# Six block pairs by eleven products, and gate products laid among the output sums, in a convolution and SwiGLU kernel

## The chip, the cores and the metric

The kernel runs on one core of one Trainium2 chip. The metric is the device time of one execution in microseconds (us). Engines are named as the profile names them: PE is TensorE's matmul stream and PEld its weight loads, DVE is VectorE, ACT is ScalarE, POOL is GpSimd, SP issues nearly all DMAs. PSUM, the memory that PE writes, is used as four pairs of banks; the code calls such a pair a duo.

## The reference, cut to what matters

```python
# x: (8, 4096, 192), weight: (8 heads, 7 taps)
w = softmax(weight, axis=-1)                     # with 1e-9 in the divisor
conv[b, s, h, g] = sum over k of w[h, k] * x_padded[b, s + k, h, g]   # causal, 6 zeros ahead
# then, with all 32768 rows of conv as tokens:
xn  = conv / sqrt(mean(conv * conv, axis=-1) + 1e-6) * rms_g
g   = xn @ w_gate                                # 192 x 1536
silu = g / (1 + exp(-g))
out = (silu * (xn @ w_val)) @ w_out              # 1536 x 192
```

All in float32. The weights arrive as float64.

## The kernel before

**Tiles and stages.** The 32768 tokens are cut into 32 *pairs* of 1024 tokens (the name `p` in the code; two groups of 512 tokens). Pair 0 and, in its gate half, pair 1 are computed by ordinary products while the weights are converted and prepared; pairs 2 to 31 run in one steady pattern. For each pair there is work ahead of the products (seven convolution taps on DVE and ACT, the norm, a turn through DRAM that puts channels on the partitions), the gate and value products, the SiLU and its multiply, and the output product.

**Gate and value products.** The 1536 hidden columns are cut into six *block pairs* `j`, each of two blocks of 128. For a block pair and the two token groups there are four results, the cells a, b, c, d. Rows 0 to 63 of the array do the gate and rows 64 to 127 the value, each with 64 of the 192 channels at a time, so a cell by the ordinary way takes three such products and the four cells take twelve. `FORM` (L71) says of each block pair which way it goes: 1 is a form with eleven products, named P1 to P7 and Q1 to Q4; 0 is the ordinary form with twelve, named Aa to Ed. Each product is six matmuls of 512 columns: three parts of a float32 operand split by hand into fp32r parts, times the two row halves (`product`, L898, issued at L910). The eleven-product form needs sums on top of the products: `f1` copies cell a to cell b in PSUM (ACT), `f3` copies cell c to two rows of the tile `tt` (ACT), `f4` and `f5` write c and d as b plus that copy (DVE, L981). P6 adds to b after `f1`; `f4` reads b after P6; P7 adds to b after `f4` has read it; `f5` reads b after P7; Q2 and P3 add to c after `f4`, Q4 to d after `f5`, Q3 and P4 to b after `f5`. Then `g` applies SiLU to a cell's gate bank (ACT, L987) and `m` multiplies by its value bank (DVE, L994).

**Output product.** It is done by seven products instead of eight for 2x2 blocks, with sums of the hidden values first (`h1` to `h4`, 24 a pair, shared between DVE and POOL, L964). For each of the seven forms and each block pair there is one step, `o1.0` to `o7.5`, 42 a pair (`step`, L918, issued at L937): six matmuls with 32 weight columns each, side by side in the array. They add up in three accumulators X, Y and Z, which a few copies, sums and transposes (`c1`, `c2`, `s7`, `C21`, `C22`, `T11` to `T22`) turn into output rows. Each accumulator took a duo of its own.

**Weights.** The prepared weight pieces of the gate stage lie in DRAM (`wd`, made by `prepare`, L733, in `NW` = 10 kinds) and come back for every pair through a ring of ten slots of 192 KB (`ring_load`, L782). A slot is loaded again as soon as its last product has been issued: 48 loads a pair.

**Order.** Nothing reorders the work: every engine does its instructions in the order in which Python issues them, and that order is written by hand. `LINE` (L111) lists PE's steps for one pair. `ORDER` (L79) is one *window* of the steady state and is run once for each pair (`run`, L1245; L1269). In `ORDER`, `p4` means the next four steps of `LINE`; a word such as `Vf4.0` means engine V (DVE; A is ACT, G is POOL, S a DMA on SP's queue) and act `f4` of block pair 0. A `+` behind a word means the next pair, `++` the one after it, `-` the pair before, nothing means the window's own pair. `cv` are the taps, `sq`, `red`, `pow`, `bc`, `mul` the norm, `x1` to `x4` sums of the split operands, `n`, `d`, `l` the splits into fp32r parts, `pl`, `ft`, `ld`, `st` the DMAs. `FIRST` (L95) is the window of pair 1 and `PLAIN` (L75) its PE steps. In a window of before, PE does the pair's P5.0 and P1.0, the last six output steps of the pair before, then the other 66 gate products of the pair in a row, then 36 of its own output steps in a row.

**Banks.** `open` (L849) takes a free duo and `give` (L857) returns it when a cell's `g` and `m` have read their halves.

Of the kernel before, what the change touches and what calls it, by code (L numbers as in the profile page):

```python
# [20 lines left out]
def kernel(  # L21
# [46 lines left out]
    SPAN = 1509  # L68
    SPLIT = 2.0**-12
    HIGH = 0xFFFFF000  # L70
    FORM = (1, 0, 1, 0, 1, 1)  # L71
    HOME = tuple(
        sum(FORM[:j]) if on else sum(FORM) + j - sum(FORM[:j]) for j, on in enumerate(FORM)
    )
    PLAIN = (  # L75
        "a0 b0 c0 d0 o1.0 a1 b1 c1 d1 o1.1 a2 b2 c2 d2 o1.2 a3 b3 c3 d3 o1.3 a4 b4 c4 d4 o1.4",
        "a5 b5 c5 d5",
    )
    ORDER = (  # L79
# [14 lines left out]
    )  # L94
    FIRST = (  # L95
# [14 lines left out]
    )  # L110
    LINE = (  # L111
# [7 lines left out]
    )  # L119

    cst = ctx.enter_context(tc.tile_pool(name="cst", bufs=1))
# [8 lines left out]
    x_sb = {}  # L130
# [30 lines left out]

    def load_part(p, h, eng):

        if h == 0:
            x_sb[p] = xs.tile([P, TB + HALO, GS], F32, name="xh")
        load_head(p, p // NB, (p % NB) * PT, h, eng)

# [505 lines left out]
    def copy(eng, dst, src):  # L673
        if eng == "A":
            nc.scalar.copy(out=dst, in_=src)  # L675
        else:
            nc.vector.tensor_copy(out=dst, in_=src)
# [32 lines left out]
    for k, (name, cols) in enumerate((("A", (0, 9)), ("B", (5, 7)), ("E", (1, 3)))):  # L710
        for c, (g, f) in CELL.items():
            OWN[name + c], RIGHTS[name + c], INTO[name + c] = (k, g), cols[f], c
    NW = 10
    NSLOT = 10

    line_of = [w.split(".") for row in LINE for w in row.split()]
# [119 lines left out]
    class Pair:  # L836
        def __init__(self, p):
            self.p = p
            self.bk, self.o_sb, self.sg = {}, {}, {}
            self.open_half, self.turned = {}, [0, 0]  # L840
            self.line = self.products()

        def hv(self, j, c):
# [13 lines left out]
        def give(self, name, n=1):  # L857
            self.open_half[name] = self.open_half.get(name, 0) + n
            if self.open_half[name] == 2:
                pool4.append(self.bk.pop(name))  # L860
                del self.open_half[name]

        def both(self, j, c):
            return duo[self.bk[j, c]][:]

        def acc(self, b):
            return duo[self.bk[b]][:, 0, :]

        def products(self):
            if self.p == 1:  # L870
# [46 lines left out]

        def step(self, form, k):  # L918
            b = ACC[form]
            if form in (1, 7) and b not in self.bk:  # L920
                full4.discard(self.open(b, False))
            fresh = form in (1, 7) and k == 0
            src = hs[:, k, :] if form == 5 else self.hv(k, LEFT[form])
            right = RIGHT[form][:, HOME[k]]
            self.tiles(b, [right[:, m] for m in range(NM)], src, fresh)
# [40 lines left out]
        def do(self, eng, name):  # L966
            act, *at = name.split(".")
            p, n = self.p, NM * P
            s5 = tt[:, 7:9, :]
            if at:  # L970
                j = int(at[0])
            if act == "f1":
                self.open((j, "b"), True)
                copy(eng, self.both(j, "b"), self.both(j, "a"))
            elif act == "f3":
                copy(eng, s5, self.both(j, "c"))
            elif act in ("f4", "f5"):
                c = "c" if act == "f4" else "d"
                if c == "d":
                    self.open((j, c), True)  # L980
                nc.vector.tensor_tensor(  # L981
                    out=self.both(j, c), in0=self.both(j, "b"), in1=s5, op=ALU.add
                )
            elif act[0] == "g":
                c = act[1]
                t = self.sg[j, c] = spots.pop(0)
                nc.scalar.activation(  # L987
                    out=tt[:, t, :], in_=self.both(j, c)[:, 0, :], func=AF.Silu
                )
                self.give((j, c))  # L990
            elif act[0] == "m":
                c = act[1]
                t = self.sg.pop((j, c))
                nc.vector.tensor_tensor(  # L994
                    out=self.hv(j, "abcd".index(c)), in0=self.both(j, c)[:, 1, :],
                    in1=tt[:, t, :], op=ALU.mult,
                )
                self.give((j, c))
                spots.append(t)
            elif act[0] == "h":  # L1000
                self.h_sum(int(act[1]), j, eng)
            elif act == "c1":
                self.open("Y", True)
                copy(eng, self.some("Y"), self.some("X"))
            elif act in ("s7", "c2"):
                i, b = (7, "Z") if act == "s7" else (8, "X")
                copy(eng, tt[:, i, 0:n], self.some(b))
            elif act in ("C22", "C21"):
                i, b = (7, "X") if act == "C22" else (8, "Z")
                t = tt[:, i, 0:n]  # L1010
                nc.vector.tensor_tensor(out=t, in0=self.some(b), in1=t, op=ALU.add)  # L1011
                if b == "Z":
                    self.give("Z", 2)
            elif act in ("T22", "T21"):
                self.turn(tt[:, 7 if act == "T22" else 8, :], 1, int(act[2]) - 1)
                self.at_end(1)
            elif act in ("T11", "T12"):
                b = "Y" if act == "T11" else "X"
                self.turn(self.acc(b), 0, int(act[2]) - 1)
                self.give(b, 2)  # L1020
                self.at_end(0)
            elif p < PAIRS - 1:
                self.leave(int(act[2]), j, eng)
# [24 lines left out]
        tap(p, k, eng)  # L1048

    def put_away(p, h, eng):  # L1050
        if h == 0:
            scr[p] = dram.tile([D, PT], F32, name="xd")
        to = scr[p][:].rearrange("(h a) (b t) -> h b a t", a=GS, t=TB)
        queue(eng).dma_start(out=to[h], in_=yn[p][h::H])
# [210 lines left out]
                    pairs[p].do(eng, name)  # L1265

    run([w for row in FIRST for w in row.split()], 1)
    for w in range(2, PAIRS + 1):
        run([w for row in ORDER for w in row.split()], w)  # L1269
# [1 line left out]
_INS = ['x', 'weight', 'moe_w_gate', 'moe_w_val', 'moe_w_out', 'moe_rms_g']  # L1271
# [26 lines left out]
```

## Time and profile before

| | before |
|---|---|
| time, median of 3 runs | 2475.02 us (2474.97 to 2477.09) |
| span of the profiled execution | 2476.6 us |
| granted PE clock over the span | 0.999 |
| instructions in the profile | 69229 |
| DMA packets, bytes | 716392, 430.55 MB |
| time of one steady window (start of a tap to the same tap one pair later) | 74.75 us |

The profiled execution's span stands 1.6 us above the median of the timed runs and inside their range. In the profile, "busy" is the time in which an engine had an instruction in flight; matmuls overlap each other, so PE's busy share tells whether PE had work, not how fast it did it. A group's row gives the busy time, the mean length of one instruction, and the idle time just before its instructions with what ended it. The chain of waits follows the work that ended last back from the end. A timeline row gives start, length, engine, line, what is written from what, and how many instructions were merged into the row.

### The profile page before, as it was taken

The numbers are of one execution on the slowest core, as the hardware profiler recorded it, in microseconds if no ns is written. First come the engines' busy times: TensorE is split into PE (matmuls) and PEld (weight loads), VectorE is DVE, ScalarE is ACT, GpSimd is POOL, SyncE is SP. The second block draws the span as 40 slices with busy tenths as digits, with TensorE's granted clock in tenths as the row PEclk, the third lists the DMA queues.
The fourth block names the chain that finished last, engine by engine and source line by source line (L and its number), as shares of the span: only waits on it lengthen the run. The fifth ranks groups of instructions, "written<-read, shape, count | busy, mean of one in ns | idle before, by whom it ended". The sixth has DMA issues, their size and how long they took to land.

```text
span 2476.6 us, 69229 instructions
## 1 busy us (share of the span) xinstructions
PE 2454.1 (99%) x29152; PEld 1896.0 (77%) x29152; DVE 2020.8 (82%) x2526; ACT 1018.0 (41%) x1435; POOL 836.2 (34%) x624
## 2 busy tenths in 40 slices
PE   8999999999999999999999999999999999999999
PEld 5546777877777877777787778777777877778777
DVE  8687888888888888888888887888888888888864
ACT  6443344434344334344334444343444343443332
POOL 0541333333333333334233434333433333333322
PEclk9999999999999999999999999999999999999999
DMA  7363677666687666786666777666776666876653
GB/s 151 60 205 107 171 200 194 190 161 175 173 205 185 189 162 173 176 211 178 177 167 171 191 193 191 173 167 172 199 198 187 160 172 172 205 185 192 159 162 94
DMA packets 716392, 430.55 MB, mean 174 GB/s; under 512 B 510330, under 2 KB 702386, under 8 KB 716082
## 3 DMA queue, kind: packets, MB, share of 16 engines
q1 hardware_dynamic: 712336, 425.21, 66.4%
q8 instruction: 230, 3.77, 0.7%
q10 hardware_dynamic: 3746, 0.92, 0.2%
q14 instruction: 80, 0.66, 0.1%
HBM read 366.96 MB, written 58.98 MB: 172 GB/s over the span
## 4 chain that ended last, share of the span: by engine, by line
PE 92%; DVE 4%; DMA 2%; issue 1%; ACT 1%; POOL 0%; SPq 0%; DVEq 0%; POOLq 0%; ACTq 0%
PE ps L910 54%; PE ps L937 35%; PE ps L882 2%; DMA xb<-xd 1%; DMA ring<-wd 1%; DVE y L445 0%; DVE ht L1109 0%; PE ps L408 0%; DVE ht L994 0%; DVE ps L981 0%; PE ps L528 0%; DVE part L345 0%; DVE part L330 0%; DVE ht L964 0%; ACT part L675 0%
## 5 line engine op out<-in xcount | busy, mean ns | idle before, releaser
L910 PE MATMUL ps<-part,ring 64*128 64x512 f32 x12240 | 1419.9, 389 | 3.4 <-DMA ring<-wd 2.3
L910 PEld LDWEIGHTS ps<-part,ring 64*128 64x128 f32 x12240 | 1151.3, 184 | 258.4 <-DVE ps L981 12.0
L987 ACT ACTIVATE tt<-ps 128x512 f32<-128x512 f32 x744 | 439.3, 599 | 714.5 <-PE ps L910 661.2
L994 DVE TENSOR_TENSOR ht<-ps,tt 128x512 f32<-128x512 f32 x744 | 497.7, 686 | 254.8 <-ACT tt L987 252.3
L937 PE MATMUL ps<-ht,wo_sb 128*32 128x384 f32 (+2 forms) x7272 | 468.3, 380 | 1.9 <-DVE tt L1011 1.1
L964 POOL TENSOR_TENSOR ht<-ht 128x512 f32<-128x512 f32 x180 | 273.6, 1527 | 541.6 <-PE ps L937 534.1
L937 PE MATMUL ps<-ht,x 128*32 128x384 f32 (+2 forms) x6696 | 440.3, 380 | 2.9 <-DVE ht L964 2.9
L937 PEld LDWEIGHTS ps<-ht,wo_sb 128*32 128x32 f32 x7272 | 325.0, 110 | 115.8 <-issue 14.8
L937 PEld LDWEIGHTS ps<-ht,x 128*32 128x32 f32 x6696 | 300.3, 110 | 93.0 <-DVE ht L964 3.1
L981 DVE TENSOR_TENSOR ps<-ps,tt 128x1024 f32<-128x1024 f32 x240 | 295.8, 1233 | 52.6 <-ACT tt L675 23.0
L445 DVE SCALAR_TENSOR_TENSOR y<-xh,tp,y 128x1536 f32<-128x1536 f32 x186 | 336.5, 1809 | 0.2
L675 ACT COPY ps<-ps 128x1024 f32<-128x1024 f32 (+1 forms) x151 | 134.6, 892 | 402.8 <-PE ps L910 326.1
L675 ACT COPY tt<-ps 128x384 f32<-128x384 f32 (+1 forms) x182 | 151.7, 834 | 225.0 <-PE ps L937 161.0
L964 POOL TENSOR_TENSOR hs<-ht 128x512 f32<-128x512 f32 x120 | 155.4, 1295 | 262.0 <-DVE ht L994 262.0
L474 POOL TENSOR_SCALAR r<-r 128x8 f32<-128x8 f32 x31 | 6.2, 199 | 509.8 <-DVE r L469 509.7
L937 PE MATMUL ps<-hs,x 128*32 128x128 f32 (+2 forms) x2232 | 161.2, 379 | 0.0
L964 DVE TENSOR_TENSOR ht<-ht 128x512 f32<-128x512 f32 x192 | 132.7, 705 | 21.3 <-PE ps L937 18.3
L937 PEld LDWEIGHTS ps<-hs,x 128*32 128x32 f32 x2232 | 106.8, 110 | 29.7
L964 DVE TENSOR_TENSOR ht<-hs,ht 128x512 f32<-128x512 f32 x156 | 112.2, 766 | 11.0 <-PE ps L937 10.2
L820 DVE SCALAR_TENSOR_TENSOR part<-part,xb 128x1024 fp32r<-128x1024 f32 x87 | 120.1, 1380 | 0.0
L818 POOL TENSOR_TENSOR part<-xb,part 128x1024 fp32r<-128x1024 f32 x29 | 69.6, 2401 | 122.3 <-PE ps L910 86.1
L495 POOL TENSOR_TENSOR xh<-y,s 128x1536 f32<-128x1536 f32 x30 | 89.9, 2997 | 15.3 <-DVE s L487 7.7
(132 smaller groups left out, 1421.1 us busy)
## 6 DMA issues: line engine op xcount, KB each, us to landing
ring<-wd SPq DMA_DIRECT2D x1440, 192.0 KB
xb<-xd SPq DMA_DIRECT2D x60, 512.0 KB
xd<-xh SPq DMA_DIRECT2D x240, 96.0 KB
xh<-in_x_dram SPq DMA_DIRECT2D x192, 105.0 KB
xb<-xd SPq DMA_DIRECT2D x60, 256.0 KB
out_dram<-o_sb SPq DMA_DIRECT2D x126, 96.0 KB
out_dram<-o_sb SPq DMA_DIRECT2D x62, 128.0 KB
wd<-part SPq DMA_DIRECT2D x5, 1152.0 KB
```

The costliest lines, as they stand in the source:

```text
L445: nc.vector.scalar_tensor_tensor(out=y, in0=xk, scalar=w, in1=y, op0=ALU.mult, op1=ALU.add)
L495: e.tensor_tensor(out=yn[p].rearrange("p a t -> p t a"), in0=y, in1=ss[:].rearrange("p (t o) -> p t o", o=1).to_broadcast([P, TB, GS]), op ...
L675: nc.scalar.copy(out=dst, in_=src)
L818: e.tensor_tensor(out=split_of(g, 1).bitcast(F32R), in0=src, in1=high, op=ALU.subtract)
L820: nc.vector.scalar_tensor_tensor(out=split_of(g, 2).bitcast(F32R), in0=high, scalar=1.0 + SPLIT, in1=src, op0=ALU.mult, op1=ALU.subtract,)
L882: nc.tensor.matmul(out=self.both(j, c)[:, h, :], lhsT=wf[HALF[h], k, 2 * HOME[j] + f, :], rhs=rb[HALF[h], k, g, :], start=(k == 0), stop=( ...
L910: nc.tensor.matmul(out=self.both(j, c)[:, h, :], lhsT=left[HALF[h]], rhs=right[HALF[h]], start=(first and q == 0), stop=True, skip_group_c ...
L937: nc.tensor.matmul(out=self.acc(b)[i * Q : (i + 1) * Q, at : at + n], lhsT=left, rhs=cols, start=fresh, stop=True, skip_group_check=True, ...
L964: engine[eng].tensor_tensor(out=dst, in0=a, in1=b, op=op)
L981: nc.vector.tensor_tensor(out=self.both(j, c), in0=self.both(j, "b"), in1=s5, op=ALU.add)
L987: nc.scalar.activation(out=tt[:, t, :], in_=self.both(j, c)[:, 0, :], func=AF.Silu)
L994: nc.vector.tensor_tensor(out=self.hv(j, "abcd".index(c)), in0=self.both(j, c)[:, 1, :], in1=tt[:, t, :], op=ALU.mult,)
```

## The change

- `FORM` is all ones: the block pairs 1 and 3 also go by eleven products, and the ordinary form is no longer used in the steady state. The tenth kind of prepared weights goes (`NW` = 9); every kind is now prepared for all six block pairs, and a pair loads 54 pieces through the ring.
- `f3` gives the duo of cell c back as soon as it has copied it, and `f4` opens a new one. The copy has three places in `tt` (rows 7 and 8, 0 and 1, 2 and 3), named by a third part of the word (`f3.1.1`).
- `settle` and `let`: accumulator Y takes the second bank of X's duo (the three accumulators take two duos instead of three).
- `LINE` and `ORDER` are new. A window now starts and ends at another place: PE does the first sixteen or so gate products of the next pair among the output steps of this one, and some output steps among the last gate products. `SECOND` is the same for pair 2. `PLAIN` takes all of pair 1's steps.
- Between the engines, per window: DVE has four `f4`/`f5` words, three `h` and two `x` words more (79 words for 70), POOL three `h` and two `x` fewer (11 for 16), ACT two `f1` and two `f3` more (46 for 42).

The lines of products and output steps move from L910 and L937 to L956 and L984.

```diff
-    FORM = (1, 0, 1, 0, 1, 1)
+    FORM = (1, 1, 1, 1, 1, 1)
...
     ORDER = (
...
+        "Aga.2 p1- Vcv1+ p1- Vmb.0 Vf4.2 p2 Vcv4+ p1- VC21- Vma.2 Agc.2 Vmc.2 p1- p2 VT12-",
+        "Vf5.2 Asq+ p1 Af3.1.1 p1 Af1.1 p1 Vred+ Gpow+ Agb.2 p2 Vmb.2 p1 Agd.2 p1 Vf4.1 Vmd.2",
...
+        "Vmb.4 p1 Vf4.5 Vh1.4 p1 Aga.5 p1 An.0+ Vh2.2 Sst0.0- p1 Sst1.4- Vh3.4 Sld.1++ Sft.5+",
+        "p3 Vh2.3 p1 Vh2.0 Agc.5 Vma.5 p2 Sld.7++ Vf5.5 Vmc.5 p1 Vx1+ Ac1 p1 Agb.5 p1 Vx3+",
+        "Vh2.1 Vh2.4 p1 Sst0.4- Vx2+ Sst0.3- p1 An.1+ Agd.5 Sst0.1- p1 Sft.4+ Vx4+ Vmb.5 p1",
+        "Vmd.5 Vl.1+ Vh1.5 p1 Vh3.5 An.3+ Vh2.5 p1 Sld.3++ p1 Vh4.0 Vd.1+ p3 Sst1.3- Sld.2++",
+        "Vd.3+ p1 Vh4.5 An.2+ Sld.4++ p3 Gl.0+ Vl.3+ p1 Ac2 Vh4.3 Vd.0+ Vd.2+ Vh4.1 p2",
+        "Sld.6++ p1 An.4+ Sld.0++ p1+ Sld.5++ Sst1.0- p1+ VT11 p1 Af3.0.1+ Gh4.4 Vl.4+ Af1.0+",
+        "Vd.4+ p2 As7 p1+ Vl.2+ Af3.2.2+ p1+ Vh4.2 p1 Vf4.0+ p1 p2+ Acv0++ p1+ Aga.0+ p1+",
+        "VC22 Vcv2++ Vma.0+ p1+ Sst1.2- p3 Vf5.0+ p1 Vcv5++ Agc.0+ p1 Vmc.0+ Vcv3++ p3+ p1",
+        "Agd.0+ Vmd.0+ Af1.2+ p2 Vcv6++ p4+ Agb.0+ Sst1.1-",
     )
...
     LINE = (
-        "P5.0 P1.0 P2.0 Q1.0 P6.0 Ab.1 Bb.1 Eb.1 P7.0 Q2.0 Aa.1 P3.0 Ea.1 Ba.1 P4.0 Q3.0 Q4.0",
...
+        "P5.0 P1.0 P5.2 P6.0 Q1.0 P2.0 Q2.0 P7.0 P3.0 Q4.0 P4.0 P1.2 Q3.0 Q1.2 P6.2 P2.2 P3.2",
+        "Q2.2 P7.2 P5.1 P1.1 P4.2 Q3.2 P6.1 Q4.2 P2.1 Q1.1 P7.1 P5.3 P3.1 Q2.1 Q4.1 P1.3 Q3.1",
+        "P4.1 P6.3 Q1.3 P2.3 P5.4 P7.3 P3.3 Q2.3 P1.4 Q3.3 P4.3 Q4.3 P6.4 Q1.4 P2.4 P5.5 P7.4",
+        "P3.4 Q2.4 P1.5 P4.4 Q4.4 Q3.4 P6.5 Q1.5 P2.5 o1.3 o1.2 o1.0 P7.5 Q2.5 P3.5 o1.4 o7.3",
+        "o1.5 o1.1 Q3.5 P4.5 Q4.5 o2.4 o2.0 o2.2 o6.0 o2.3 o2.5 o7.2 o7.4 o6.2 o6.5 o7.5 o6.4",
+        "o2.1 o6.1 o6.3 o7.0 o7.1 o5.3 o5.1 o5.5 o5.4 o5.2 o5.0 o3.4 o3.0 o4.0 o4.2 o4.4 o3.2",
+        "o3.5 o4.3 o4.1 o4.5 o3.1 o3.3",
     )
...
-    NW = 10
+    NW = 9
...
+        def fork(self, j):
+            return tt[:, self.s5[j] : self.s5[j] + 2, :]
...
+        def settle(self, b):
+
+            x = self.at.get("X")
+            if b != "X" and x and not any(v == (x[0], 1) for v in self.at.values()):
+                self.at[b] = x[0], 1
+                return
+            i = self.open(b, b != "Z")
+            if b != "Y":
+                full4.discard(i)
+            self.at[b] = i, 0
+
+        def let(self, b):
+            i, _ = self.at.pop(b)
+            if all(v[0] != i for v in self.at.values()):
+                self.give(next(n for n in "XYZ" if self.bk.get(n) == i), 2)
...
             elif act == "f3":
-                copy(eng, s5, self.both(j, "c"))
+                self.s5[j] = (7, 0, 2)[int(at[1])] if at[1:] else 7
+                copy(eng, self.fork(j), self.both(j, "c"))
+                self.give((j, "c"), 2)
             elif act in ("f4", "f5"):
                 c = "c" if act == "f4" else "d"
-                if c == "d":
-                    self.open((j, c), True)
+                self.open((j, c), True)
                 nc.vector.tensor_tensor(
-                    out=self.both(j, c), in0=self.both(j, "b"), in1=s5, op=ALU.add
+                    out=self.both(j, c), in0=self.both(j, "b"), in1=self.fork(j), op=ALU.add
                 )
...
     run([w for row in FIRST for w in row.split()], 1)
-    for w in range(2, PAIRS + 1):
+    run([w for row in SECOND for w in row.split()], 2)
+    for w in range(3, PAIRS + 1):
         run([w for row in ORDER for w in row.split()], w)
```

More of the change, by code (lines that the diff above doesn't have):

```diff
@@ L76 @@
         "a0 b0 c0 d0 o1.0 a1 b1 c1 d1 o1.1 a2 b2 c2 d2 o1.2 a3 b3 c3 d3 o1.3 a4 b4 c4 d4 o1.4",
-        "a5 b5 c5 d5",
[3 rows of a table added]
     )
     ORDER = (
[14 rows of a table removed]
[16 rows of a table added]
+    )
+    SECOND = (
[17 rows of a table added]
     )
@@ L162, in load_part @@
     def load_part(p, h, eng):
-        if h == 0:
+        if p not in x_sb:
             x_sb[p] = xs.tile([P, TB + HALO, GS], F32, name="xh")
@@ L840, in __init__ @@
             self.open_half, self.turned = {}, [0, 0]
+            self.begun = set()
+            self.s5 = {}
+            self.at = {}
             self.line = self.products()
@@ L861, in give @@
                 del self.open_half[name]
+        def fork(self, j):
+            return tt[:, self.s5[j] : self.s5[j] + 2, :]
         def both(self, j, c):
             return duo[self.bk[j, c]][:]
+        def settle(self, b):
[11 more added lines that the diff above has]
+                self.give(next(n for n in "XYZ" if self.bk.get(n) == i), 2)
         def acc(self, b):
-            return duo[self.bk[b]][:, 0, :]
+            i, h = self.at[b] if b in self.at else (self.bk[b], 0)
+            return duo[i][:, h, :]
         def products(self):
@@ L919, in step @@
             b = ACC[form]
-            if form in (1, 7) and b not in self.bk:
-                full4.discard(self.open(b, False))
-            fresh = form in (1, 7) and k == 0
+            if b not in self.at:
+                self.settle(b)
+            fresh = (b not in self.begun) and form in (1, 7)
+            self.begun.add(b)
             src = hs[:, k, :] if form == 5 else self.hv(k, LEFT[form])
@@ L968, in do @@
             p, n = self.p, NM * P
-            s5 = tt[:, 7:9, :]
             if at:
@@ L1002, in do @@
             elif act == "c1":
-                self.open("Y", True)
+                self.settle("Y")
                 copy(eng, self.some("Y"), self.some("X"))
@@ L1012, in do @@
                 if b == "Z":
-                    self.give("Z", 2)
+                    self.let("Z")
             elif act in ("T22", "T21"):
@@ L1019, in do @@
                 self.turn(self.acc(b), 0, int(act[2]) - 1)
-                self.give(b, 2)
+                self.let(b)
                 self.at_end(0)
@@ L1050, in put_away @@
     def put_away(p, h, eng):
-        if h == 0:
+        if p not in scr:
             scr[p] = dram.tile([D, PT], F32, name="xd")
```

61 rows, old and new, of tables (FIRST, LINE, ORDER, PLAIN) are left out of this document.

## The prediction

> **What bounds the kernel now.** I read the page's first part, then a table of three stretches of one window's length (74.75 us), then the chain of waits over two windows, and last the single rows where the chain changes its kind.
>
> ```profile
> PE 2454.1 (99%) x29152; PEld 1896.0 (77%) x29152; DVE 2020.8 (82%) x2526; ACT 1018.0 (41%) x1435; POOL 836.2 (34%) x624
> PE 92%; DVE 4%; DMA 2%; issue 1%; ACT 1%; POOL 0%; SPq 0%; DVEq 0%; POOLq 0%; ACTq 0%
> ```
> ```profile
> core 0: us, PE busy (x) PEld busy (x) DVE busy (x) ACT busy (x) POOL busy (x), PEclk, DMA share, GB/s
> 1199.60:1274.35 74.75, 74.75 (x914) 58.61 (x914) 62.18 (x76) 30.86 (x42) 26.33 (x19) 1.00 0.69 182
> 1274.35:1349.10 74.75, 74.40 (x904) 60.85 (x908) 61.99 (x76) 31.08 (x42) 27.20 (x19) 1.00 0.71 182
> 1349.10:1423.85 74.75, 74.75 (x918) 58.66 (x914) 62.89 (x77) 30.91 (x43) 25.99 (x19) 1.00 0.70 182
> ```
>
> PE is busy in every steady window from end to end at full granted clock; DVE has 62.4 of 74.75 us, ACT 31, POOL 26.5. PE busy alone could hide waits, so the waits are looked at by themselves:
>
> ```profile
> PE ps L910 <- DMA ring<-wd: 2.3, 3, 1.0
> PEld ps L910 <- DVE ps L981: 12.0, 29, 0.6
> PEld ps L910 <- ACT ps L675: 4.5, 29, 0.2
> PE ps L937 <- DVE ht L964: 2.9, 1, 2.9
> ```
>
> Over the whole span PE's products waited 2.3 us for weights and PE's output steps 2.9 us for DVE. The weight loads waited 12 us for `f4`/`f5` and 4.5 for a copy by ACT, but the matmuls behind them did not. So in the steady state the time of a window is the sum of PE's own steps, and only what changes that sum, or what makes PE wait anew, changes the end.
>
> **The price of PE's steps.** The chain of waits over one window, with start and length:
>
> ```profile
> 1199.59 45.59 PE ps L910 x396
> 1245.18 23.54 PE ps L937 x288
> 1268.72 1.59 PE ps L910 x12
> 1270.31 4.04 PE ps L937 x48
> ```
>
> The first row is 66 gate products in a row (6 matmuls each), the second 36 output steps in a row, the third the two products P5.0 and P1.0, the fourth the last six output steps. Long against short runs separate the price of a step from the price of beginning a run. Products: (45.59 - 1.59) / 64 = 0.6875 us each, so the short run holds 1.59 - 2 x 0.6875 = 0.215 us that belongs to no product. Output steps: (23.54 - 4.04) / 30 = 0.65 us each, and 4.04 - 6 x 0.65 = 0.14 us over. A change from products to output steps and back thus costs 0.355 us. A second place bears this out, the window of pair 1, where single output steps stand between long runs of ordinary products (starts in the first column):
>
> ```profile
> 160.05 0.86 PE L937 MATMUL ps<-ht,wo_sb 128*32 128x384 f32 x12
> 160.84 10.62 PE L882 MATMUL ps<-xb,part 64*128 64x512 f32 x48
> 171.39 0.86 PE L937 MATMUL ps<-ht,wo_sb 128*32 128x384 f32 x12
> 172.18 10.57 PE L882 MATMUL ps<-xb,part 64*128 64x512 f32 x48
> ```
>
> From the start of a lone output step to the next product it is 160.84 - 160.05 = 0.79 and 172.18 - 171.39 = 0.79 us: 0.65 + 0.14 again. The rows also show what changes: products are of the kind 64*128 (two row halves), output steps 128*32 (four column strips).
>
> The Trainium skill, "TensorEngine Tiling (Array Packing)", section "Key Properties", says that changing the tiling mode, and not merely the tile, drains TensorE; this case's trace agrees, with 0.355 us for two such changes. "TensorE: Matmul & The Clock Gate", section "Single matmul latency", gives the part of a matmul's latency that does not depend on its length as about 166 ns warm; twice that is an estimate of 0.33 us, and by it the sum below would end some 5 us lower.
>
> **The change part by part.**
>
> *Two products fewer a pair.* Block pairs 1 and 3 go from 12 to 11: 66 instead of 68, for pairs 2 to 31. 30 x 2 x 0.6875 = -41.3 us. This lies wholly on the path.
>
> *Runs of PE.* Before, a window has 2 runs of products (P5.0 P1.0, and the 66): 30 x 2 = 60 in all. After, reading the `p` words of the new `ORDER` with `LINE`, the runs of products between output steps are: P5.0 P1.0; P5.2 P6.0; Q1.0 to P3.0; Q4.0 P4.0 P1.2; Q3.0 to P2.2; P3.2 Q2.2; P7.2 to P2.5; P7.5 Q2.5 P3.5; Q3.5 P4.5 Q4.5. That is 9 a window, in 29 windows; the last pair's window has 4, as no next pair is there. 29 x 9 + 4 = 265, or 205 more. 205 x 0.355 = +72.8 us. No other engine can cover it, since PE itself does nothing in it. A window of after by these prices: 66 x 0.6875 + 42 x 0.65 + 9 x 0.355 = 75.9 us; of before, 68 x 0.6875 + 42 x 0.65 + 2 x 0.355 = 74.8, as measured.
>
> Bounds of the price of a run: the short run of products stands beside the one weight load that waited for DVE,
>
> ```profile
> 1268.65 1.23 PEld L910 LDWEIGHTS ps<-part,ring 64*128 64x128 f32 x12 [0.20 <-issue]
> 1270.24 3.84 PEld L937 LDWEIGHTS ps<-ht,wo_sb 128*32 128x32 f32 x72 [0.36 <-DVE o_sb L952]
> 1274.28 1.70 PEld L910 LDWEIGHTS ps<-part,ring 64*128 64x128 f32 x16 [0.20 <-issue]
> ```
>
> with 0.36 instead of 0.20. If all 0.16 were such a wait, a run would cost 0.195 us, and the change 205 x 0.195 - 41.3 = -1 us. But the lone steps of pair 1, with no such wait near, have the same 0.14 on their side, so I take 0.355 and hold 0.30 for the lowest likely (+20 us).
>
> *DVE.* Added per window: four `f4`/`f5`, three `h`, two `x`. Lengths and spacings from the timeline and the page:
>
> ```profile
> 1201.97 1.23 DVE L981 TENSOR_TENSOR ps<-ps,tt 128x1024 f32<-128x1024 f32 x1
> 1203.12 0.68 DVE L994 TENSOR_TENSOR ht<-ps,tt 128x512 f32<-128x512 f32 x1
> 1209.09 2.47 DVE L994 TENSOR_TENSOR ht<-ps,tt 128x512 f32<-128x512 f32 x4
> 1252.36 2.49 DVE L964 TENSOR_TENSOR ht<-hs,ht 128x512 f32<-128x512 f32 x4
> 1261.12 1.81 DVE L445 SCALAR_TENSOR_TENSOR y<-xh,tp,y 128x1536 f32<-128x1536 f32 x1
> 1262.85 1.21 DVE L818 TENSOR_TENSOR part<-xb,part 128x1024 fp32r<-128x1024 f32 x1
> 1263.98 1.81 DVE L445 SCALAR_TENSOR_TENSOR y<-xh,tp,y 128x1536 f32<-128x1536 f32 x1
> 1271.32 1.15 DVE L952 STREAM_TRANSPOSE o_sb<-tt 128x256 f32<-128x256 f32 x4
> ```
>
> Start to start an `f4` takes 1.15, an `h` or `m` 0.62 (2.49 / 4), a tap 1.73, a split 1.13. 4 x 1.15 + 5 x 0.62 = 7.7, so DVE has 62.4 + 7.7 = 70 of 75.9 us: 5.8 us idle instead of 12.4. It is no bound by its sum, but may be late where its work is thick. The thickest stretch runs from the moment DVE waits for PE (`m` of cell d of block pair 5, after Q4.5) to the moment PE waits for DVE (P3.2, after `f4` of block pair 2). PE's steps in it: 33 output steps, 16 products and 11 changes at half of 0.355, 21.5 + 11.0 + 2.0 = 34.4 us. DVE's: five `m` and eight `h` at 0.62, nine splits at 1.13, three `f` at 1.15, five taps at 1.73, and a transpose pair and a sum of some 0.5 each, 31.4 us, and 1.7 us ahead of it for the SiLU of d, which stands behind a split on ACT. 33.1 against 34.4: DVE comes in time by 1.3 us. Had the runs cost nothing, it would have been late by 0.7. So the cover is there, but thin; a DVE that needs 2 us more than this in the stretch would add 0.7 us a window, 20 us in all.
>
> *ACT and POOL.* Four more copies and three `h`, two `x` fewer:
>
> ```profile
> L675 ACT COPY tt<-ps 128x1024 f32<-128x1024 f32 x120 | 121.9, 1016 | 64.1 <-DVE o_sb L952 33.3 <-PE ps L910 30.7
> L964 POOL TENSOR_TENSOR hs<-ht 128x512 f32<-128x512 f32 x120 | 155.4, 1295 | 262.0 <-DVE ht L994 262.0
> ```
>
> ACT goes to 31 + 4 x 1.02 = 35 us, POOL to 26.5 - 5 x 1.3 = 20 us; both lie under PE. The tightest place is a copy of a to b with two products (1.38 us) between P1 and P6, a copy of 1.0 us; block pair 4 of before stood so too, and there the weight load waited 4.5 / 29 = 0.16 us and the matmul not. Where another copy comes just ahead (block pair 1), P6 may wait 0.1 to 0.2 us, up to 6 us in all. I set nothing for it and keep it in the range.
>
> *Banks.* Returning c early and laying Y beside X sets free the duos that the next pair's first products need; without it the runs among the output steps could not be there. It takes no time of its own.
>
> *Ring and SP.* 54 loads a pair for 48, 30 x 6 x 192 KB = 35 MB more on 430.55. Ring slots come free at least nine products (6.2 us) ahead of the first use in both orders. DMA share would go from 0.70 to about 0.75. On SP's queue ring loads stand behind output and `pl` DMAs for some tenths of a us, less than that lead. Nothing.
>
> *Start and end.* Preparing nine kinds for six block pairs is 54 blocks for 48; it lies beside pair 1's products, which fill that stage:
>
> ```profile
> 90.00:200.00 110.00, 106.89 (x1034) 58.13 (x1030) 83.31 (x98) 39.32 (x65) 57.33 (x44) 1.00 0.50 142
> ```
>
> At the end two transpose pairs (`T22`, `T21`) come behind the last `T12`: +1.15 us by the row of four transposes above.
>
> Sum: -41.3 + 72.8 + 1.2 = +32.7 us. On the median, 2475.0 + 32.7 = 2508 us (on the profiled span 2509).
>
> **The rivals.**
>
> Forecast, chance 0.75: PE stays the bound and pays for the runs; 2495 (0.30 a run) to 2525 (with 0.5 us a window of small waits).
>
> DVE or ACT late in the thick stretch, chance 0.16: for it speaks that DVE is left only 5.8 us a window and that its operations on two SBUF operands can lengthen while POOL works, as this sum does (`x1`, 1.49 us, beside its like of 0.69); against it that POOL has a quarter less to do.
>
> ```profile
> 1394.25 1.49 DVE L832 TENSOR_TENSOR tt<-xb 128x512 f32<-128x512 f32 x1
> 1395.77 0.69 DVE L832 TENSOR_TENSOR tt<-tt,xb 128x512 f32<-128x512 f32 x1
> ```
>
> Four such meetings in the thick stretch eat 3.2 us, of which 1.3 are free: with 0.7 to 1.5 us a window on top it is 2525 to 2555.
>
> The product run is cheaper in the new order, chance 0.04: 0.195 us a run, 2475, no change.
>
> The other side, chance 0.05: changing between the two kinds costs nothing where the next weights are loaded early; the 0.355 would then be the waits of those four places alone. Then -41.3 and DVE's lateness of 0.7 a window, +20: 2455. Two of the lone steps of pair 1 with the same 0.14 speak against it. It decides from a price of a run below 0.2 us.
>
> **How the numbers follow.** A measurement of this kernel can tell about 0.2%, 5 us, from no change. Faster: 0.05; the same: 0.03; slower: 0.92. The range of 8 in 10 goes from 2490 to 2535: it leaves out the far half of the late DVE and the two cheap cases.
>
> **What would show it.** A steady window of 75.5 to 76.5 us, with PE busy throughout, 11880 product matmuls (for 12240), and 9 runs of products in the chain of a window; short runs in it that hold 0.2 us more than their products; DVE at about 70 us of a window with idle left. The forecast is wrong if short runs show 0.69 us a product, if the window is under 75 us, or if PE's products or weight loads wait 0.5 us or more a window for DVE or ACT.

## The result and the profile after

The changed kernel takes 2662.56 us (median of 4 runs, 2658.68 to 2671.8), the kernel before beside it 2474.99 us (4 runs, 2474.35 to 2477.09): 1.0761 times as long, 95% interval 1.0741 to 1.0781. The prediction had 2508 us and at most 2535. The direction was right; the loss is 187.6 us where 33 was forecast.

The first part of the page of after (busy time, share of the span, instructions):

```profile
PE 2550.2 (96%) x28792; PEld 1831.6 (69%) x28792; DVE 2258.2 (85%) x2792; ACT 1143.3 (43%) x1553; POOL 598.7 (22%) x475
```

PE falls from 99% to 96%, though it has 360 matmuls fewer: it now waits. Where, in the span, one marker shows: each window has one `pow` of the norm on POOL. The next two rows are that instruction in the timeline of one line, for before and for after, from 240 us on (count, shortest/median/longest ns, first and last start):

```profile
L474 POOL TENSOR_SCALAR r<-r x29: 197/198/200, 241.0 to 2337.8; 128x8 f32<-128x8 f32 x29
```
```profile
L497 POOL TENSOR_SCALAR r<-r x29: 196/196/200, 263.4 to 2521.6; 128x8 f32<-128x8 f32 x29
```

28 windows take 2258.2 us for 2096.8, so a mean window is 80.65 us for 74.88. The profiled spans differ by 2670.0 - 2476.6 = 193.4 us: 161.4 in these windows, 22.4 ahead of them, 9.6 behind, where the same waits go on to the last pair. Two consecutive windows of after, as a table of stretches (busy times with instructions, then granted PE clock and DMA share):

```profile
core 0: us, PE busy (x) PEld busy (x) DVE busy (x) ACT busy (x) POOL busy (x), PEclk, DMA share, GB/s
1200.00:1279.12 79.12, 75.24 (x866) 55.02 (x860) 68.64 (x81) 33.13 (x44) 17.76 (x14) 1.00 0.69 184
1279.12:1361.00 81.88, 77.98 (x902) 57.19 (x902) 71.70 (x86) 35.07 (x46) 18.07 (x14) 1.00 0.69 180
```

The windows come in two lengths, near 79.1 and near 81.9 us; the clock is full and DVE has the 70 us that were forecast. By the prediction's prices a window is 75.9 us. The timeline of PE over most of a long window of after (start, length, line, matmuls; in brackets idle time of PE before the row and what ended it) shows what came on top. In these rows a product counts six matmuls and an output step twelve, though the code issues six for a step; the chain of waits counts eight of them.

```profile
1220.71 0.86 PE L984 MATMUL ps<-ht,wo_sb 128*32 128x384 f32 x12
1222.28 0.86 PE L984 MATMUL ps<-ht,wo_sb 128*32 128x384 f32 x12 [0.71 <-DVE tt L1058]
1223.07 30.74 PE L956 MATMUL ps<-part,ring 64*128 64x512 f32 x252
1253.74 2.16 PE L984 MATMUL ps<-ht,wo_sb 128*32 128x384 f32 x36
...
1258.12 0.86 PE L984 MATMUL ps<-ht,wo_sb 128*32 128x384 f32 x12
...
1260.78 1.51 PE L984 MATMUL ps<-ht,wo_sb 128*32 128x384 f32 x24 [1.15 <-DVE ht L1041]
1262.22 2.34 PE L956 MATMUL ps<-part,ring 64*128 64x512 f32 x18
1264.49 2.16 PE L984 MATMUL ps<-ht,wo_sb 128*32 128x384 f32 x36
...
1271.81 2.16 PE L984 MATMUL ps<-ht,x 128*32 128x384 f32 x36 [1.26 <-DVE ht L1011]
...
1276.51 1.51 PE L984 MATMUL ps<-ht,x 128*32 128x384 f32 x24 [0.60 <-ACT tt L698]
...
1278.60 1.66 PE L956 MATMUL ps<-part,ring 64*128 64x512 f32 x12
1280.18 2.16 PE L984 MATMUL ps<-hs,x 128*32 128x384 f32 x36
```

The price of a run stands as forecast: the two products at 1278.60 take 1.58 us to the next step, 0.205 over 2 x 0.6875. Over the forecast there are four things, each from start to start:

- two output steps with the wait for `C21`: 1223.07 - 1220.71 = 2.36 for 2 x 0.65 + 0.14, so 0.92 us;
- the 42 products in a row: 30.67 for 42 x 0.6875 + 0.215 = 29.09, so 1.6 us, with no idle time of PE in it;
- the 18 output steps from 1264.49: 14.11 for 11.84. Of the 2.27, some 0.8 belong to the wait for the copy `c2` (0.60 of idle, and the restart);
- in the long windows alone the other 1.5 of those 2.27, and the four steps from 1258.12, 4.10 for 2.74: 1.36 more. Both wait for DVE.

The first three make 3.3 us, the last 2.85: 79.1 and 82 us. What the 42 products lose is seen in the weight loads. Before, over its 66 products (in brackets the time that the load waited, and for what):

```profile
1199.52 10.08 PEld L910 LDWEIGHTS ps<-part,ring 64*128 64x128 f32 x90 [0.20 <-issue]
1209.83 16.91 PEld L910 LDWEIGHTS ps<-part,ring 64*128 64x128 f32 x150 [0.23 <-DVE ht L994]
1226.89 15.53 PEld L910 LDWEIGHTS ps<-part,ring 64*128 64x128 f32 x138 [0.15 <-ACT ps L675]
1242.82 1.93 PEld L910 LDWEIGHTS ps<-part,ring 64*128 64x128 f32 x18 [0.39 <-DVE ps L981]
```

After, in its 42:

```profile
1225.36 1.23 PEld L956 LDWEIGHTS ps<-part,ring 64*128 64x128 f32 x12 [0.38 <-DVE ps L1028]
1226.86 2.59 PEld L956 LDWEIGHTS ps<-part,ring 64*128 64x128 f32 x24 [0.27 <-ACT ps L698]
1229.77 2.58 PEld L956 LDWEIGHTS ps<-part,ring 64*128 64x128 f32 x24 [0.32 <-DVE ps L1028]
1232.69 2.62 PEld L956 LDWEIGHTS ps<-part,ring 64*128 64x128 f32 x24 [0.34 <-ACT tt L698]
...
1238.49 4.65 PEld L956 LDWEIGHTS ps<-part,ring 64*128 64x128 f32 x42 [0.44 <-DVE ps L1028]
1243.40 2.61 PEld L956 LDWEIGHTS ps<-part,ring 64*128 64x128 f32 x24 [0.25 <-ACT ps L698]
1246.58 4.67 PEld L956 LDWEIGHTS ps<-part,ring 64*128 64x128 f32 x42 [0.57 <-DVE ps L1028]
1251.49 1.90 PEld L956 LDWEIGHTS ps<-part,ring 64*128 64x128 f32 x18 [0.24 <-ACT ps L698]
```

Before has three breaks behind the first row, after one for nearly every sum `f1` (ACT) and `f4`, `f5` (DVE). And the start, on PE and on DVE of after, ahead of the first product from the ring (L956):

```profile
235.80 5.52 PE L984 MATMUL ps<-ht,wo_sb 128*32 128x384 f32 x60 [9.56 <-DVE tt L1058]
241.25 1.65 PE L956 MATMUL ps<-part,ring 64*128 64x512 f32 x12
```
```profile
229.76 5.52 DVE L468 SCALAR_TENSOR_TENSOR y<-xh,tp,y 128x1536 f32<-128x1536 f32 x3
235.19 0.55 DVE L1058 TENSOR_TENSOR tt<-ps,tt 128x384 f32<-128x384 f32 x1
```

In before the same product starts at 219.24 us, with the last six output steps of pair 1 behind it; in after five of them (3.4 us) stand ahead. So the start is 18.6 us late, and half of that is the wait of 9.56 us of those five for the sum `C22`, which stands on DVE behind taps at the end of pair 1's window.

### The profile page after: what moved, and what is told of

The parts are those of the page before. It is cut to its first block, busy times and chain, and to the rows that moved or that the text cites. A ratio compares the mean times of both kernels' runs of the same rounds, so it can differ in the third digit from the quotient of the medians.

```text
span 2670.0 us, 69577 instructions
## 1 busy us (share of the span) xinstructions
PE 2550.2 (96%) x28792; PEld 1831.6 (69%) x28792; DVE 2258.2 (85%) x2792; ACT 1143.3 (43%) x1553; POOL 598.7 (22%) x475
## 5 line engine op out<-in xcount | busy, mean ns | idle before, releaser
L956 PE MATMUL ps<-part,ring 64*128 64x512 f32 x11880 | 1480.9, 398 | 9.2 <-DVE ps L1028 2.7
L956 PEld LDWEIGHTS ps<-part,ring 64*128 64x128 f32 x11880 | 1088.7, 185 | 340.3 <-DVE ps L1028 54.3
L984 PE MATMUL ps<-ht,wo_sb 128*32 128x384 f32 (+2 forms) x7272 | 461.5, 384 | 47.3 <-DVE tt L1058 31.6
L1028 DVE TENSOR_TENSOR ps<-ps,tt 128x1024 f32<-128x1024 f32 x360 | 443.8, 1233 | 66.6 <-PE ps L956 26.0
L984 PE MATMUL ps<-ht,x 128*32 128x384 f32 (+2 forms) x6696 | 418.1, 381 | 40.9 <-DVE ht L1011 21.3
L984 PEld LDWEIGHTS ps<-ht,wo_sb 128*32 128x32 f32 x7272 | 296.6, 110 | 209.6 <-issue 69.6
L984 PEld LDWEIGHTS ps<-ht,x 128*32 128x32 f32 x6696 | 293.0, 110 | 145.5 <-ACT tt L698 27.5
L698 ACT COPY tt<-ps 128x384 f32<-128x384 f32 (+1 forms) x242 | 212.4, 878 | 319.0 <-PE ps L956 157.9
L698 ACT COPY ps<-ps 128x1024 f32<-128x1024 f32 (+1 forms) x211 | 194.5, 922 | 160.6 <-DVE ht L1041 98.2
L1011 POOL TENSOR_TENSOR ht<-ht 128x512 f32<-128x512 f32 x150 | 193.1, 1305 | 154.0 <-PE ps L984 149.2
L698 ACT CAST part<-xb 128x1024 fp32r<-128x1024 f32 x87 | 90.9, 1045 | 192.6 <-DMA xb<-xd 192.6
L1011 DVE TENSOR_TENSOR ht<-hs,ht 128x512 f32<-128x512 f32 x186 | 155.2, 861 | 9.2 <-PE ps L984 7.5
L1011 POOL TENSOR_TENSOR hs<-ht 128x512 f32<-128x512 f32 x90 | 116.6, 1296 | 182.4 <-DVE ht L1041 180.4
L984 PE MATMUL ps<-hs,x 128*32 128x128 f32 (+2 forms) x2232 | 140.0, 382 | 0.6 <-ACT tt L698 0.6
L984 PEld LDWEIGHTS ps<-hs,x 128*32 128x32 f32 x2232 | 93.5, 110 | 49.7 <-issue 20.9
```

The costliest lines, as they stand in the source:

```text
L956: nc.tensor.matmul(out=self.both(j, c)[:, h, :], lhsT=left[HALF[h]], rhs=right[HALF[h]], start=(first and q == 0), stop=True, skip_group_c ...
L984: nc.tensor.matmul(out=self.acc(b)[i * Q : (i + 1) * Q, at : at + n], lhsT=left, rhs=cols, start=fresh, stop=True, skip_group_check=True, ...
L1011: engine[eng].tensor_tensor(out=dst, in0=a, in1=b, op=op)
L1028: nc.vector.tensor_tensor(out=self.both(j, c), in0=self.both(j, "b"), in1=self.fork(j), op=ALU.add)
```

## The experiments

The theory after the first look: the price of a run is right, and the rest is waits, which come from the shared duo, from sums too close to their products, and from a meeting of DVE and POOL. The rival: DVE, with 70 us of work a window, is simply full.

**e1, before with one run more.** A steady window of before does P5.0 and P1.0 three steps apart:

```diff
-        "p2 Vl.2 VC22- VT11- p3- Vd.4 ...
+        "p1 Vl.2 VC22- VT11- p3- p1 Vd.4 ...
```

> The kernel of before with one thing moved: three of the six output steps of the pair before stand between P5.0 and P1.0, the other three behind P1.0. The work is the same, a window has three runs of products instead of two. If a change of kind on PE costs 0.36 us a run whatever stands around it: 30 x 0.36 = +11 us, 2486 us. If the price of a run was only the waits of its particular places (rival): within 3 us of 2475. In the trace each of the two short runs of one product should take about 0.9 us from start to the next step's start (0.69 + 0.22).

2491.98 us (2487.55 to 2493.26, 5 runs), ratio 1.0066 (1.0052 to 1.0079), +17.0 us or 0.57 a run. PE's timeline:

```profile
1276.03 0.96 PE L910 MATMUL ps<-part,ring 64*128 64x512 f32 x6
1277.06 2.16 PE L937 MATMUL ps<-ht,wo_sb 128*32 128x384 f32 x36
1279.15 0.96 PE L910 MATMUL ps<-part,ring 64*128 64x512 f32 x6
1280.04 2.16 PE L937 MATMUL ps<-ht,wo_sb 128*32 128x384 f32 x36
```

The second lone product takes 0.89 us to the next step, 0.20 over 0.6875; three output steps take 2.09, 0.14 over 1.95. The first product takes 1.03: 0.14 more, as the step behind it waits 0.50 us for its weights (for the sum `C22`) where the step behind the second waits 0.36. In the traces the median window goes from 74.74 to 75.20 us: 0.34 for the run and 0.14 for that wait, 14 of the 17 us; the other 3 were not found. So 0.355 a run holds, and the rival of a cheap run is out.

**e2, after without taps.** All six `Vcv` words leave the window, 10 us of DVE's work; the norm and what follows then work on other values.

> The changed kernel without the six convolution taps of DVE in the steady windows (only the tap of ACT is left, so the convolution is incomplete): 10.4 us less DVE work a window. If the new waits of PE are DVE coming late because it is full (theory DVE): nearly all of them go, windows of about 77 us, time near 2550. If they are distances in PE's own order that are too short for the chain PE, DVE or ACT, PE (theory distance), and waits for work on the other half of a shared duo: the long run of 42 products still holds 1.5 us or more over its products, the two waits of about 0.9 and 0.6 us on the summing work of the output product stay, windows of about 79 us, time 2600 to 2625; only the waits that come in half of the windows (h and m, 2.7 us) may go.

2664.57 us (one run). Windows of 79.1 and 81.9 us and the same four waits as in after. The long windows stayed too (9 of 28 near 82 us, for 13 in after), so the time lies above the 2600 to 2625 us that were expected. DVE's load is not the cause in after.

**e3, no step beside a reader of its duo.** It is X and Z, not X and Y as the section on the change has it, that share a duo in the steady state: `o7.3` opens Z before `c1` opens Y, and `settle` gives the bank beside X to whichever comes first. `C21` and `c2` read one bank of it while PE's next step writes the other. The edit moves the reader or the step:

```diff
-  ... p1- VC21- Vma.2 Agc.2 Vmc.2 p1- p2 VT12- ...
+  ... p1- Vma.2 Agc.2 Vmc.2 p1- VC21- p2 VT12- ...
-        "o2.1 o6.1 o6.3 o7.0 o7.1 ...
+        "o6.1 o6.3 o2.1 o7.0 o7.1 ...
```

> The changed kernel with two things moved: the sum C21, which reads accumulator Z, goes behind the last output step of X (o3.3) instead of between o3.1 and o3.3; and o2.1, a step on accumulator Y, goes between o6.3 and o7.0. X and Z lie in the two halves of one duo. If an access to one half waits for the other half's (theory shared duo): the waits of 0.9 us (PE for C21) and 0.6 us (PE for the copy of X, c2) a window go, 29 x 1.5 = 43 us, about 2620 us. If those waits are for something else (rival: DVE and ACT late for their own reasons): within 10 us of 2662.

2616.4 us (2613.61 to 2622.29, 4 runs), ratio 1.0575 (1.0561 to 1.059): 46 us less than after. Windows are 77.57 and 80.38 us, and both waits are gone.

**e4, DVE and POOL apart.** In a long window of after DVE, POOL and ACT stand so:

```profile
1256.62 3.50 DVE L1011 TENSOR_TENSOR ht<-hs,ht 128x512 f32<-128x512 f32 x2
```
```profile
1257.18 2.39 POOL L841 TENSOR_TENSOR part<-xb,part 128x1024 fp32r<-128x1024 f32 x1 [7.99 <-ACT part L698]
```
```profile
1256.06 1.05 ACT L698 CAST part<-xb 128x1024 fp32r<-128x1024 f32 x1 [1.60 <-DMA xb<-xd]
```

ACT's split of operand 0 waits for the fetch of `xb`; POOL's split `l.0` follows it and falls on two `h` sums of DVE, which take 3.50 us. The edit gives the split to DVE, in `ORDER` and in `SECOND`:

```diff
-  ... p3 Gl.0+ Vl.3+ ...
+  ... p3 Vl.0+ Vl.3+ ...
```

> The changed kernel with the split l.0 on DVE instead of POOL. In half of the windows it starts while DVE does h sums on two SBUF operands, these take 3.5 us for two instead of 1.3, and PE then waits 1.15 and 1.25 us for m and h. If that meeting makes the slow half of the windows (theory meeting): all windows at about 79.1 us or a little more for 1.14 us of DVE work, some 13 to 16 windows x 2.8 = 36 to 45 us less, 2615 to 2630. If the slow windows come from DVE being too full (rival): no gain or a loss, 2655 to 2690.

2632.02 us (2630.35 to 2633.01, 4 runs), ratio 1.0634 (1.062 to 1.0649): 30.5 us less. Nearly every window takes 79.1 to 79.2 us, and the pair of sums reads in DVE's timeline:

```profile
1242.37 1.29 DVE L1010 TENSOR_TENSOR ht<-hs,ht 128x512 f32<-128x512 f32 x2
```

So the meeting makes the long windows. The Trainium skill, "SBUF — State Buffer", section "Who interferes with whom", says that a DVE instruction with two SBUF inputs contends with a GpSimd instruction that reads SBUF; the trace agrees, with 3.50 us against 1.29.

**e5, the three mended.** e3, e4, and the taps at the start taken out of the way of `C22`:

```diff
     FIRST:
-  ... Vh4.4 Vcv2++ Vd.4+ Vl.2+ Vcv5++ Vcv3++ Vcv6++
+  ... Vh4.4 Vd.4+ Vl.2+
     SECOND:
-  ... VT21- p2- ... Vma.0 p1 Vf5.0 Agc.0 Vmc.0 p3 ...
+  ... VT21- Vcv2+ Vcv5+ p2- ... Vma.0 Vcv3+ p1 Vf5.0 Agc.0 Vmc.0 Vcv6+ p3 ...
```

> The changed kernel with the two moves of the run e3 (C21 behind o3.3, o2.1 behind o6.3), the split l.0 on DVE as in e4, and at the start three taps of the next pair moved behind C22 and the transposes of pair 1, where PE waited 9.6 us for C22 behind them. If the three causes are separate and add up: all windows at 77.6 us, 2616 - 13 x 2.8 - 9 = 2571 us. What is left against before is then the seven more runs (2.5 us a window) and the short waits in the long run of products (1.6 us), less two products (1.4 us). If the mended waits only uncover others behind them (rival): above 2590.

2589.35 us (2588.45 to 2593.06, 4 runs), ratio 1.0467 (1.0452 to 1.0483). 73 us less than after, 18 short of what was expected. The first product of the ring comes at 233.94 us, 7.3 earlier, and a steady window takes 77.92 us, 0.35 more than e3's short ones: the run of five products in it holds 0.55 us over its products where after's holds 0.2, behind `f4.0`. A wait has come in the place of those that left.

**e6, the sums half as long.** e5 with `f1`, `f3`, `f4` and `f5` on half of their columns, so that half of b, c and d lacks them:

```diff
-                copy(eng, self.both(j, "b"), self.both(j, "a"))
+                copy(eng, self.both(j, "b")[:, :, 0 : T // 2], self.both(j, "a")[:, :, 0 : T // 2])
```

> As e5, but f1, f3, f4 and f5 work on half of each bank's columns (the other half of the results is then left wrong): each takes about half its time. The order and the number of instructions are the same. If the long run of 42 products is 1.85 us over its products because the chain product, f1 or f4 or f5, product is longer than the products between allow (theory distance): the excess falls below 0.8 us, windows of 76.5 us or less, about 2535 us. If it is for something else, as bank turnover by SiLU and multiply (rival): the excess stays above 1.4 us, windows of 77.3 us or more, 2560 us.

2528.02 us (one run). Its weight loads in the long run (from the edge of the view on), and the chain of waits from that run over the window behind it:

```profile
1016.82 24.45 PEld L954 LDWEIGHTS ps<-part,ring 64*128 64x128 f32 x215
```
```profile
1015.84 25.85 PE ps L954 x228
1041.69 2.09 PE ps L982 x24
...
1088.57 5.47 PE ps L954 x45
```

No break is left, and the chain is PE alone. The shortest windows take 75.7 us; the prediction's prices gave 75.9. So the sum was right for PE and wrong for what PE waits on. The chain's first row gives the length of a product without waits: 25.85 us for 38 products, 0.680 each. Beside it the 66 products of before, at 0.6875, hold some 0.5 us of waits, and the 42 of after 1.9.

**e8, fewer runs.** e5 with the last four output steps among the others (P3.2 behind P1.1), seven runs a window for nine:

```diff
-  ... Vmd.0+ Af1.2+ p2 Vcv6++ p4+ Agb.0+ ...
+  ... Vmd.0+ Af1.2+ p6 Vcv6++ VC21 VT12 p4+ Agb.0+ ...
-  "... P6.2 P2.2 P3.2", "Q2.2 P7.2 P5.1 P1.1 P4.2 ...
+  "... P6.2 P2.2 P1.1", "P3.2 Q2.2 P7.2 P5.1 P4.2 ...
```

> As e5, but the last four output steps of a pair stand with its others ahead of Q3.0 and no longer among P3.2 to P7.2, and P1.1 goes ahead of P3.2: 7 runs of products a window instead of 9. By the price of a run alone: 2 x 0.36 = 0.7 us a window less, 76.9 us, 2550 us. But the output steps were also what stood between P6.2 and P3.2, where f4 needs some 1.7 us: two products (1.4 us) are left there, and P1.1 must wait for the transposes. If the steps between earned their price (rival): no gain, 77.6 us or more a window.

2720.22 us (one run), 131 over e5. PE's timeline at the place from which the steps went:

```profile
1000.38 4.38 PE L954 MATMUL ps<-part,ring 64*128 64x512 f32 x36 [1.39 <-DVE ps L1026]
1007.87 23.81 PE L954 MATMUL ps<-part,ring 64*128 64x512 f32 x198 [3.12 <-DVE ps L1026]
```

1.39 and 3.12 us of PE's time go to sums that the output steps had covered. Over the span PE waits 138.8 us for `f4` and `f5`, for 6.9 in e5: the whole loss. The runs among the output steps buy something: at this place far more than their price.

**e9, before with a shared duo.** Z in the second bank of X's duo, nothing else:

```diff
-            return duo[self.bk[b]][:, 0, :]
+            return duo[self.bk["X"]][:, 1, :] if b == "Z" else duo[self.bk[b]][:, 0, :]
```

> The kernel of before with one part of the change alone: accumulator Z lies in the second half of X's duo. Nothing is copied or multiplied more or less. If steps on one half wait for reads of the other half (theory shared duo): o4.3 behind c2, o7.5 behind c1, and C21 behind o5.5 cost PE 0.6 to 1 us a window, 20 to 30 us, 2495 to 2507. If sharing is free (rival): within 4 us of 2475.

2541.33 us (2539.79 to 2542.88, 4 runs), ratio 1.0268 (1.0251 to 1.0285), 67 us more, over twice what was expected. PE's timeline over the last 30 of the 36 output steps that stand in a row:

```profile
1200.01 0.86 PE L937 MATMUL ps<-ht,x 128*32 128x384 f32 x12
...
1204.03 1.51 PE L937 MATMUL ps<-ht,wo_sb 128*32 128x384 f32 x24 [0.56 <-ACT ps L675]
...
1212.16 0.86 PE L937 MATMUL ps<-ht,x 128*32 128x384 f32 x12 [0.62 <-ACT tt L675]
...
1221.40 1.66 PE L910 MATMUL ps<-part,ring 64*128 64x512 f32 x12
```

In every window PE stands still for `c1` and for `c2`, 17.5 and 19.4 us over the span. The 30 steps take 21.39 us for 19.64, and the last six steps of the pair, behind `C21`, hold 0.3 us more than in before, which is most of the 67 us in 30 windows. In a window of before with X, Y and Z apart there is none of this.

**e10, the wait of e5 taken away.** `f4` of the next pair's block pair 0 ahead of a sum of `h` on DVE:

```diff
-  ... p1+ Vh4.2 p1 Vf4.0+ p1 p2+ ...
+  ... p1+ Vf4.0+ Vh4.2 p1 p1 p2+ ...
```

> e5_three_mended with one word moved: f4 of the next pair's block pair 0 stands ahead of h4.2 on DVE instead of behind it. In e5 the run of five products held 0.56 us more than its products where the same run of after held 0.19, and its weight load waited 0.46 us for that f4, which stands behind l.0, the split that e4 and e5 moved from POOL to DVE. Theory (the wait moved along: DVE, now without its meeting with POOL, is late at f4.0 by the split it took over): an h takes 0.62 us of DVE, more than the 0.46, so the run falls to 0.2 over its products, a window from 77.92 to 77.55 us, the kernel from 2589 to about 2579. Rival (f4.0 waits for PE's own product and not for DVE's queue): no change, 2589.

2589.65 us (2588.55 to 2592.03, 4 runs): nothing gained. The run of five products falls from 3.99 to 3.66 us as expected, but two runs later PE waits again, ahead of P3.2. DVE, and PE, of e10:

```profile
1101.34 3.66 DVE L466 SCALAR_TENSOR_TENSOR y<-xh,tp,y 128x1536 f32<-128x1536 f32 x2
1104.92 0.68 DVE L1039 TENSOR_TENSOR ht<-ps,tt 128x512 f32<-128x512 f32 x1
1105.71 1.23 DVE L1026 TENSOR_TENSOR ps<-ps,tt 128x1024 f32<-128x1024 f32 x1
```
```profile
1105.28 1.51 PE L982 MATMUL ps<-ht,x 128*32 128x384 f32 x24
1107.04 1.66 PE L954 MATMUL ps<-part,ring 64*128 64x512 f32 x12 [0.25 <-issue]
```

`f4.2` ends at 1106.94, 0.1 us before P3.2 starts, and DVE has had no pause ahead of it. The profile calls this wait "issue"; the times tell whose it is.

**e11, e10 without taps.**

> e10_f4_ahead with the six taps that DVE does in a window left out (the norm and all behind it then work on other values). In e10 the wait before f4.0 is gone, but the window stays at 77.95 us and the wait stands one product run later: from 1098.4 to 1106.9 us DVE works without a pause (f4.0's two taps, m, f5.0, taps, m, f4.2), and the product behind f4.2 starts 0.1 us after f4.2 ends, with 0.25 us of idle. Theory (with the other waits mended, DVE's queue is what sets this stretch, as the prediction's thick stretch had it): without the taps f4.2 ends over 3 us earlier, the 0.32 us go, and the window comes to 77.55 to 77.65 us, the kernel to about 2578. It does not come lower, as the waits of the long run for its own sums stay. Rival (f4.2 waits for a product, a bank or ACT): the window stays at 77.95.

2581.69 us (one run), with most windows at 77.6 us. DVE was late there, by some 0.35 us a window, and no more: the rest of e10's excess over 75.7 stays when DVE has 10 us less to do.

## Why the prediction was right and wrong

- *What bounds before, two products fewer, the price of a run*: right, but for one reading. The prediction says of the weight loads that waited in before that "the matmuls behind them did not". By e6's 0.680 us a product they did, by some 0.5 us a window, and that is hidden in the price of 0.6875. In after a run of products holds 0.2 us and the run of output steps behind it 0.15 over its steps, and e6, which keeps all nine runs, has the forecast window. By these terms alone 33 of the 187.6 us are explained.
- *"Banks ... It takes no time of its own"*: wrong. Two accumulators in one duo made PE wait for the readers of the other bank. Taking the two steady waits out of after is worth 46 us (e3); putting such sharing into before costs 67 (e9). The prediction looked at which duos come free and not at who reads the bank beside the one that is written.
- *"I set nothing for it"* (copies of ACT close to their products, with DVE's sums beside them): wrong. It took before's 0.16 us at the weight load, which it read as free, for the rule. In after the sums of six block pairs follow one another with no ordinary products between (no run puts such products back), the loads wait 0.24 to 0.57 us each, and the 42 products lose 1.6 us a window against the prediction's price. The prediction's own sign of being wrong shows: loads of products wait 54.3 us over the span for `f4` and `f5`, 1.9 a window. Halving the sums takes 61 us from e5 (e6), and e11 shows that it is not their load on DVE: 10 us a window less of that gave 8 us in all. What counts is the length of the chain from a product over its sum to the next. Banks are likely a part of it, as a sum that opens a duo (`f4` does so now) can have to wait for an `m` that frees one: ahead of its copies `f1` ACT sits idle 48.2 us for an `m` over the span of after, and 0.8 in before. What this part alone costs has no run of its own.
- *"Ring and SP ... Nothing"*: right for the weights (PE's products wait 1.3 us for them over the span, and the DMA share of a window is 0.69, under the forecast 0.75), wrong for what else SP carries. The fetch of `xb` lands late for ACT's split of operand 0, which waits for it 0.7 to 3.8 us in every one of the 28 windows, where before has a few such waits of 1.4 us at most. So POOL's `l.0` comes among DVE's `h` sums. The long windows are not those in which the fetch lands latest: in 13 windows ACT's split starts 27.6 to 28.5 us behind the marker, one of the two sums starts beside `l.0` and takes 2.9 us, and the window takes 82. In 12 it starts at 28.6 to 29.6, `l.0` starts behind the start of both sums, each takes 0.7, and the window takes 79.1 (one 79.8). In the other three it starts behind 30 and the window takes near 81, for a reason that was not looked into. Taking the meeting away is worth 30.5 us (e4). The prediction's second rival had this lengthening of DVE beside POOL, but in the thick stretch; it stands ahead of it. Why the landing varies was not settled.
- *DVE "in time by 1.3 us"*: its load was right at 70 us; with PE delayed by the other waits it was in time (e2). With three waits mended it was late by 0.35 us (e5, e10, e11), 1.65 from the forecast; but e5 had given DVE the split `l.0`, 1.13 us, so the margin itself was too large by only some 0.5 us.
- *"Start and end"*: wrong. Pair 1's window was costed by the products that fill it, but its end was reordered: 18.6 us, of which e5 won 7 back.

Together: e5 removes 73 us, halved sums another 61, and 2528 us is left, 53 over before for the 33 of the sum; the other 20 are the rest of the start and some windows of e6 over 75.7 (their mean is 76.0). The range failed because each unknown wait was bounded by what before showed of its like, and in after several of them fall into one window.

## What to carry to other kernels

A product that is saved by adding sums removes PE work and adds a chain; ordinary products that look wasteful may be the cover of such chains, and their price is known only when they are gone. Before filling gaps with work of another tiling mode, divide the saving by the price of a mode change: here a window without waits takes 66 x 0.6875 + 42 x 0.65 = 72.7 us and 0.355 a run, so against 74.75 it breaks even at fewer than six runs, and nine could not have won; none of the versions run here beats the kernel before. When two users get halves of one buffer, list every reader of one half that stands next to a writer of the other.

## What the runs showed of the hardware

- A weight load that waits slows the products without idle time of PE: eight waits in the long run of after add up to 2.8 us (0.24 to 0.57 each), and the run takes 1.9 us more than 42 products at e6's 0.680. On the mean all but some 0.11 us of each reaches PE. Over the whole span, PE's own waits for those sums read 2.7 us.
- An idle time that the profile shows for PE is less than what it costs. In the long window of after the two output steps from 1220.71 lose 0.92 us with 0.71 of idle, and the four from 1258.12 lose 1.36 with 1.15: 0.21 more each time. That is by how much the row of a lone step (0.86) is longer than the distance from step to step (0.65).
- PE's step waits for a reader of the other bank of the same duo. The waiting matmul carries a wait for the reader's semaphore and starts 0.05 us behind the reader's end (`c2` ends at 1276.46 us in after, the step starts at 1276.51), so the program asks for it. Whether the chip would need it, no run here tells.
